# A table of 4722 queue edits laid over a planned two-layer attention and mixer kernel

## The chip, the core and the metric

The kernel runs on one core of a Trainium2 chip. The metric is the device time of one execution in microseconds. Inputs are given, outputs are one bf16 array of 2048 x 448.

## The reference

Sequence 2048, width 448, 16 heads of 28. Two blocks A and B, each applied twice with the same weights:

```python
def A(x):                                   # attention
    q, k, v = split(x @ wqkv)               # 16 heads of 28
    p = softmax(q @ k.T * 28 ** -0.5)
    return (p @ v) @ wo
def B(x):                                   # token mixer and MLP
    h = gelu(layernorm(x) @ w1)
    hs = shift_tokens_by_quarter(h) @ w2    # quarters moved by -1, +1, -2, +2 tokens
    x1 = x + hs
    return x1 + gelu(layernorm(x1) @ w3) @ w4      # 448 -> 1792 -> 448
x = x + A(layernorm(x)); x = x + B(layernorm(x))   # and both once more
```

## The kernel before, in words

Nothing in this kernel stands in a fixed program order. Some sixty small generators (`t_load`, `t_kv`, `t_scores`, `t_exp`, `t_pv`, `t_norm`, `t_outproj`, `t_mixA`, `t_mixB`, `t_w4` and so on) each yield operations with an engine, a planned duration, and the tiles that they read and write. `Sched.run` plays these against planned durations on the host while the kernel is built, and always records next the operation that it would start first; that record is a `Plan`. The order of a queue on the chip is the order in which its operations were recorded. `Plan.add` derives what each operation depends on, `Plan.finalize` turns that into semaphore waits, and `Plan.emit` writes the five queues (`pe`, `act`, `dve`, `pool`, `sp`). The plan has 11344 operations: 8083 on PE, 893 on ACT, 1552 on DVE, 454 on POOL and 362 on SP, which issues the DMAs.

The steps that matter here:

- **Scores** (`score_ops`, L1423). Queries are taken in chunks of 512 or 256 columns, keys in tiles of 128, heads in four groups of four. One score matmul multiplies a 28-wide (padded to 32) slice of keys with the queries; head j of a group lies in partitions 32j to 32j+31, so the matmul uses 32 rows of the array and all 128 columns, at `tile_position=(32 * j, 0)`. PSUM has eight banks. Score blocks go to banks 0, 1 and 2 for one unit and 3 and 4 for the next, in turn.
- **Exponentials** (`t_exp`, L1661). ACT takes a unit's three banks (1536 columns) or two banks (1024 columns) in one instruction and writes the tile `PT`. The scores of a unit wait until the unit before the last has been read out of its banks. Some blocks are sent to DVE instead, which makes the exponential in five steps (L1505, L1532, L1534, L1536, L1539; 97 blocks).
- **P times V** (`t_pv`, L819 through the helper `mm`). One matmul per key tile and head: 128 rows, and 32 columns of the array, its result in partitions 32j to 32j+31 of bank 5. The loop that records them has the head innermost:

```python
for kb in batch:
    for i, kt in enumerate(kbs[kb]):
        for j in range(4):
            yield op("pe", ..., mm(ps[32 * j:32 * j + 32, 5, 0:NW], vaug[...], buf[...], ...,
                                   tile_position=(0, 32 * j)), ...)
```

- **All other products** (L828 through the helper `mm4`): projections of q, k and v, the output projection, w1 to w4. Each operation emits four matmuls, one for each group of 32 columns.
- **Filler** (`keep_pe_busy`, L2151): 1006 operations of four matmuls on `ident`, put into PE's queue where the planner saw PE idle for long.
- On ACT besides the exponentials: the table changes and gelu of the MLP (L2105), tanh for the mixer's gelu (L1925), scale factors (L1368). On DVE: evacuation of PSUM, normalization, the update of the queries between key segments (L1445). On POOL: squares and normalization factors. On SP: weights, the round trips of the unnormalized output (`uscr`, `ub`), the broadcast of the reciprocal sums (`rscr`, `fb`), DMA transposes (L1038) and the output rows (L2140, two buffers `obf`).

Near the end, after the last exponential, there remain the last chunk's output projection and MLP: w3 and w4 products of 14 tiles, gelu on ACT and the output rows.

Of the kernel before, what the change touches and what calls it, by code (L numbers as in the profile page):

```python
# [13 lines left out]
U16 = mybir.dt.uint16  # L14

ENGS = ("pe", "act", "dve", "pool", "sp")


class _Op:
    __slots__ = ("eng", "fn", "deps", "sig", "cnt", "waits", "dma", "ekey", "vc", "sem", "t_end", "pos", "plan")  # L20

    def __init__(self, eng, fn, dma):
        self.eng = eng
        self.fn = fn
        self.deps = {}
        self.sig = False
        self.cnt = 0
        self.waits = ()
        self.dma = dma
        self.ekey = ("dma", id(self)) if dma else eng  # L30
        self.vc = None
        self.sem = None
        self.t_end = 0.0
        self.pos = 0


def _split(acc):
    if isinstance(acc, tuple) and len(acc) == 2 and isinstance(acc[0], tuple):
        return acc
    return acc, None  # L40


class Plan:
    def __init__(self):
        self.ops = {e: [] for e in ENGS}
        self.all = []
        self.track = {}
        self.listen = {}
        self.dirty = set()

    def deps(self, eng, reads, writes, extra=(), dma=False):
        out = {}

        def dep(d):
            if d is None:
                return
            if eng == "pe" and d.eng == "pe" and not d.dma and not dma:
                return
            cur = out.get(d.ekey)
            if cur is None or d.pos > cur.pos:  # L60
                out[d.ekey] = d

        for d in extra:
            dep(d)
        track = self.track
        for is_write, accs in ((False, reads), (True, writes)):
            for acc in accs:
                if len(acc) == 2 and type(acc[0]) is tuple:
                    key, part = acc
                else:  # L70
                    key, part = acc, None
                st = track.get(key)
                if st is None:
                    continue
                wl, rl = st
                psum = key[0] == "ps"
                for (o2, p2) in wl:
                    if part is None or p2 is None or part == p2 or (psum and (o2.eng != eng or o2.dma or dma)):
                        dep(o2)
                if is_write or psum:  # L80
                    for (o2, p2) in rl:
                        if (is_write and (part is None or p2 is None or part == p2)) or (psum and (o2.eng != eng or o2.dma or dma)):
                            dep(o2)
        return out

    def add(self, eng, fn, reads=(), writes=(), deps=(), dma=False, t_end=0.0):
        op = _Op(eng, fn, dma)
        op.pos = len(self.all)
        op.t_end = t_end
        op.deps = self.deps(eng, reads, writes, deps, dma)  # L90
        for is_write, accs in ((False, reads), (True, writes)):
            for acc in accs:
                key, part = _split(acc)
                st = self.track.get(key)
                ls = self.listen.get(key)
                if ls:
                    self.dirty |= ls
                if st is None:
                    st = self.track[key] = ([], [])
                wl, rl = st  # L100
                if is_write:
                    if part is None:
                        del wl[:]
                        del rl[:]
                    else:
                        wl[:] = [(o2, p2) for (o2, p2) in wl if p2 != part]
                        rl[:] = [(o2, p2) for (o2, p2) in rl if p2 != part]
                    wl.append((op, part))
                else:
                    rl[:] = [(o2, p2) for (o2, p2) in rl if not (o2.ekey == op.ekey and p2 == part)]  # L110
                    rl.append((op, part))
        self.ops[eng].append(op)
        self.all.append(op)
        return op

    def finalize(self, nc, stack):
# [3 lines left out]
        sems = {}  # L120
        for e in ENGS:
            sems[e] = stack.enter_context(nc.semaphore("sem_" + e))
            c = 0
            for op in self.ops[e]:
                if not op.dma and op.sig:
                    c += 1
                    op.cnt = c
                    op.sem = sems[e]
        known = {e: {} for e in ENGS}
        pool = []  # L130
# [54 lines left out]
class Sched:  # L185
# [12 lines left out]
    def __init__(self, P):  # L198
        self.P = P
        self.cur = {e: 0.0 for e in ENGS}  # L200
        self.runq = []
# [391 lines left out]
def build_kernel(nc, A_x, A_wqkv, A_wo, B_x, B_w1, B_w2, B_w3, B_w4, out, n_layers=2):  # L593
# [13 lines left out]
    NKV = 23  # L607
# [68 lines left out]
    P = Plan()  # L676
    SC = Sched(P)
    st = contextlib.ExitStack()
    with st:
        def sb(name, shape, dt):  # L680
            return st.enter_context(nc.sbuf_tensor(name, shape, dt))

        ps = st.enter_context(nc.psum_tensor("ps", [128, 8, 512], FP32))
        x_res = sb("x_res", [128, XR, D], FP32)
        obf = sb("obf", [128, 2, D], BF16)
        ones_bf = sb("ones_bf", [128, 128], BF16)
# [37 lines left out]
        vaug = sb("vaug", [128, NKV, 512], BF16)  # L724
# [58 lines left out]
        def op(eng, dur, fn, reads=(), writes=(), **kw):  # L783
            if eng == "pool" or (eng == "dve" and kw.pop("two", False)):
                kw["port"] = True
            if eng == "dve" and dur > 0.3:
                dur += 0.008
            return (eng, dur, fn, list(reads), list(writes), kw)
# [93 lines left out]
        def t_setup():  # L882
            yield op("dve", 0.1, lambda e: e.memset(ones_f[:, :], 1.0), writes=[("ones_f",)])
            yield op("dve", 0.15, lambda e: e.memset(ones_bf[:, :], 1.0), writes=[("ones_bf",)])
            yield ("spawn", t_setup_pool(), 0)
            yield ("spawn", t_setup_act(), 0)
            yield ("spawn", t_setup_ind(), 0)
            yield op("dve", 0.06, lambda e: e.memset(halfs[:, :], 0.5), writes=[("halfs",)])
            yield op("dve", 0.06, lambda e: e.memset(neghalf[:, :], -0.5), writes=[("neghalf",)])
            yield op("dve", 0.2, lambda e: e.memset(xn[:, :, D:512], 0.0), writes=[(("xn", i), "pad") for i in range(NXN)])  # L890
            yield ("sig", ("setup",))
            for (wp, nm) in ((wk_pad, "wk_pad"), (wq_pad, "wq_pad")):
                yield op("dve", 0.2, lambda e, wp=wp: e.memset(wp[:, :, :].rearrange("p c (h r) -> p c h r", r=32)[:, :, :, 28:32], 0.0), writes=[((nm,), "p")])
                yield op("dve", 0.27, lambda e, wp=wp: e.memset(wp[64:128, 3, :], 0.0), writes=[((nm,), "p")])
                yield ("spawn", t_pack(0 if nm == "wq_pad" else 1), 0)
            yield ("spawn", t_setup_late(), 2)
            yield ("spawn", t_setup2(), 4)
            yield ("spawn", t_ratio(), -1)
# [39 lines left out]
        def t_setup_act():  # L938
            pads = vaug[:, :, :].rearrange("p t (h r) -> p (t h) r", r=32)
            yield op("act", 1.4, lambda e: e.activation(out=pads[:, :, 28:32], in_=ones_bf[:, 0:4].unsqueeze(1).to_broadcast([128, 16 * NKV, 4]), func=ACT.Copy, scale=0.0),  # L940
                     reads=[("ones_bf",)], writes=[("vaug_all",)])
            yield op("act", 0.45, lambda e: e.activation(out=pads[:, :, 28:29], in_=ones_bf[:, 0:1].unsqueeze(1).to_broadcast([128, 16 * NKV, 1]), func=ACT.Copy),
                     reads=[("ones_bf",)], writes=[("vaug_all",)])
            yield ("sig", ("vinit",))

        wsts = [PT[:, 0:4, 0:D], PT[:, 4:8, 0:D]]
# [1248 lines left out]
        SC.spawn(t_final(), 9)  # L2195
        est = SC.run()

        P.finalize(nc, st)
        with nc.Block() as block:
            @block.sync  # L2200
# [23 lines left out]
def bass_interleave_layers__mha_block__mixer_s_mlp__prompt_kernel(nc, A_x, A_wqkv, A_wo, B_x, B_w1, B_w2, B_w3, B_w4, out):  # L2224
    build_kernel(nc, A_x, A_wqkv, A_wo, B_x, B_w1, B_w2, B_w3, B_w4, out)
# [28 lines left out]
```

## Time and profile before

| what | value |
|---|---|
| median of 3 runs | 1028.84 us (1028.56 to 1029.57) |
| profiled execution, its own time | 1027.68 us |
| span of that execution | 1026.0 us |
| granted TensorE clock | 1.000 throughout |
| first score matmul, last score matmul | 15.1 us, 973.45 us after the start |
| ACT, idle time in the windows from 25 to 950 us | 2.4 us |
| DMA | 62.64 MB, 61 GB/s mean |

The span is from the first to the last instruction of the profiled execution; its own time is taken by the device around that. Line numbers in the profile are those of the kernel before; in the changed kernel the same statements stand 678 lines lower (L819 is L1497, L828 is L1506, L1423 is L2101, L1661 is L2339; the filler's L2151 is L2829). PE is the matmuls, PEld the weight loads that go with them; both are issued from one queue. "x790" is a count of instructions, and a group's busy time counts overlapping instructions once.

### The profile page before, as it was taken

To read this page: it belongs to the slowest core of one execution; us is meant where nothing else is said; L and a number is where in the kernel's file an instruction comes from. 1 tells how busy PE (TensorE), PEld (TensorE's weight loads), DVE (VectorE), ACT (ScalarE), POOL (GpSimd) and SP (SyncE) were. 2 spreads that over 40 slices of the span, in tenths; PEclk is the share of its full clock that TensorE was granted. 3 is DMA by queue.
4 is the path that set the end of the run, shared out by engine and by line. 5 is a ranking of instruction groups with operands and counts; after the bars stand their busy time and mean duration, and the time that the engine had idled before them with its cause. 6 is when DMAs were issued, how large, how long until landed. Compare 5 with 4: busy or idle time off the path is not lost.

```text
span 1026.0 us, 37152 instructions
## 1 busy us (share of the span) xinstructions
PE 989.0 (96%) x16783; PEld 428.8 (42%) x16785; DVE 804.5 (78%) x1552; ACT 988.5 (96%) x907; POOL 289.6 (28%) x458
## 2 busy tenths in 40 slices
PE   8999999999999999999999999999999999999998
PEld 4332444444333244444433343433434443444465
DVE  8868899988888776876777687987897887786551
ACT  8999999999999999999999999999999999999952
POOL 3313011531433205242335122112534140522130
PEclk9999999999999999999999999999999999999999
DMA  4633242310221003121222024433302120121000
GB/s 126 150 108 112 73 107 71 63 39 24 55 66 44 12 23 99 29 59 28 49 88 60 12 81 127 136 85 94 71 24 38 44 43 13 34 69 31 13 16 29
DMA packets 99398, 62.64 MB, mean 61 GB/s; under 512 B 68712, under 2 KB 88552, under 8 KB 99240
## 3 DMA queue, kind: packets, MB, share of 16 engines
q1 hardware_dynamic: 99240, 60.27, 22.9%
q8 instruction: 131, 2.15, 0.9%
q14 instruction: 27, 0.22, 0.1%
HBM read 28.16 MB, written 16.76 MB: 44 GB/s over the span
## 4 chain that ended last, share of the span: by engine, by line
ACT 63%; PE 32%; DVE 3%; DMA 1%; issue 1%; POOL 0%; SPq 0%; DVEq 0%; ACTq 0%
ACT PT L1661 57%; PE ps L828 16%; PE ps L1423 8%; PE ps L819 5%; PE ps L2151 2%; ACT h2T L2105 2%; ACT fb L1925 1%; DMA fb<-rscr 1%; DVE fb L1532 1%; ACT L2105 1%; ACT L1661 1%; ACT kT L2105 0%; DMA PT<-in_A_wqkv_dram 0%; DVE fb L1534 0%; ACT vaug L2105 0%
## 5 line engine op out<-in xcount | busy, mean ns | idle before, releaser
L1661 ACT ACTIVATE PT<-ps 128x1024 bf16<-128x1024 f32 (+1 forms) x790 | 894.0, 1311 | 2.9 <-PE ps L1423 1.3
L1423 PE MATMUL ps<-qT,kT 32*128 32x512 bf16 (+1 forms) x2304 | 272.9, 335 | 17.4 <-ACT PT L1661 12.2
L819 PE MATMUL ps<-PT,vaug 128*32 128x512 bf16 (+1 forms) x2445 | 246.7, 341 | 0.0
L828 PE MATMUL ps<-xT,w 128*32 128x512 bf16 (+4 forms) x2816 | 187.7, 340 | 2.1 <-DVE h2T L2084 0.7
L2151 PE MATMUL ps<-ident 128*32 128x256 bf16 x4024 | 179.2, 277 | 1.7 <-POOL ident L913 1.5
L1423 PEld LDWEIGHTS ps<-qT,kT 32*128 32x128 bf16 x2304 | 70.8, 91 | 246.2 <-ACT PT L1661 219.7
L2151 PEld LDWEIGHTS ps<-ident 128*32 128x32 bf16 x4024 | 116.3, 97 | 34.0 <-issue 13.7
L819 PEld LDWEIGHTS ps<-PT,vaug 128*32 128x32 bf16 x2445 | 73.1, 95 | 90.2 <-issue 76.9
L828 PEld LDWEIGHTS ps<-xT,w 128*32 128x32 bf16 (+1 forms) x2816 | 77.1, 95 | 54.8 <-issue 24.6
L1505 DVE TENSOR_SCALAR yd<-ps 128x512 int32<-128x512 f32 x93 | 63.9, 687 | 23.3 <-PE ps L1423 22.6
L1768 POOL TENSOR_TENSOR otn<-ub,fb 128x512 bf16<-128x512 f32 (+1 forms) x28 | 33.2, 1187 | 157.8 <-DMA fb<-rscr 150.0
L828 PE MATMUL ps<-w,h2T 128*32 128x448 bf16 x1120 | 75.7, 354 | 0.9 <-ACT h2T L2105 0.4
L1532 DVE SCALAR_TENSOR_TENSOR fb<-yd 128x512 f32<-128x512 uint16 x93 | 70.9, 768 | 0.7
L1534 DVE SCALAR_TENSOR_TENSOR fb<-fb,yd 128x512 f32<-128x512 f32 x93 | 68.1, 735 | 0.5
L2084 DVE CAST h2T<-ps 128x512 bf16<-128x512 f32 (+1 forms) x71 | 45.1, 635 | 27.7 <-PE ps L828 26.6
L1539 DVE SCALAR_TENSOR_TENSOR PD<-yd,PD 128x512 int16<-128x512 int16 x93 | 64.4, 694 | 1.4
L1161 POOL TENSOR_TENSOR sq<-kT 128x512 bf16<-128x512 bf16 (+2 forms) x32 | 32.4, 1018 | 93.9 <-DVE kT L1175 82.3
L1161 POOL TENSOR_TENSOR sq<-qT 128x512 bf16<-128x512 bf16 x24 | 27.6, 1154 | 105.1 <-DVE qT L1220 99.9
L828 PE MATMUL ps<-xT,wq_pad 128*32 128x512 bf16 x512 | 44.9, 382 | 0.6 <-issue 0.5
L1536 DVE TENSOR_SCALAR PD<-fb 128x512 bf16<-128x512 f32 x94 | 41.6, 444 | 0.8
L828 PE MATMUL ps<-wo_pad,otn 128*32 128x448 bf16 x512 | 37.5, 355 | 4.1 <-DVE vaug L2077 1.6
L1423 PE MATMUL ps<-wk_pad,kT 32*128 32x512 bf16 x256 | 39.2, 385 | 1.8 <-ACT PT L1661 1.4
(196 smaller groups left out, 1227.0 us busy)
## 6 DMA issues: line engine op xcount, KB each, us to landing
uscr<-ub SPq DMA_DIRECT2D x28, 256.0 KB
ub<-uscr SPq DMA_DIRECT2D x28, 256.0 KB
fb<-rscr SPq DMA_DIRECT2D x24, 256.0 KB
xnd<-xn SPq DMA_DIRECT2D x28, 128.0 KB, 2.5
xd<-x_res SPq DMA_DIRECT2D x16, 224.0 KB, 3.9
x_res<-xd SPq DMA_DIRECT2D x16, 224.0 KB
w<-in_B_w_dram SPq DMA_DIRECT2D x5, 448.0 KB, 8.2
obf<-in_A_x_dram SPq DMA_DIRECT2D x16, 112.0 KB
```

The lines of the kernel that those rows point to most:

```text
L819: return lambda e: e.matmul(out=out, lhsT=lhsT, rhs=rhs, start=start, stop=stop, **kw)
L828: r.append(e.matmul(out=out[c:c + w, :], lhsT=lhsT[:, c:c + w], rhs=rhs, start=start, stop=stop, tile_position=(0, c)))
L1161: return both("sq", 0.15 + NW * 0.0018, 0.07 + NW * 0.00104, lambda e: e.tensor_tensor(out=sq[:, si, 0:NW], in0=src, in1=src, op=ALU.mult) ...
L1423: yield op("pe", (0.005 + NW * 0.00042) / nc_, lambda e, i=i, kc=kc, j=j, g=g, qt=qt, a=a, NW=NW, bank=bank: e.matmul(out=ps[:, bank, i * ...
L1505: yield op("dve", c_ps(512), lambda e: e.tensor_scalar(out=y, in0=ps[:, bi(bank), :], scalar1=SCALE * L2E * FS, scalar2=-126.0 * FS, op0=A ...
L1532: yield op(D_[0][0], D_[0][1], lambda e: e.scalar_tensor_tensor(out=q, in0=lo, scalar=E2 / E3 * FS, in1=lo, op0=ALU.add, op1=ALU.mult), re ...
L1534: yield op(D_[1][0], D_[1][1], lambda e: e.scalar_tensor_tensor(out=q, in0=q, scalar=E1 / E3 * FS * FS, in1=lo, op0=ALU.add, op1=ALU.mult) ...
L1536: yield op(D_[2][0], D_[2][1], lambda e: e.tensor_scalar(out=pdt, in0=q, scalar1=E3 / FS ** 3, scalar2=E0, op0=ALU.mult, op1=ALU.add), rea ...
L1539: yield op(D_[3][0], D_[3][1], lambda e: e.scalar_tensor_tensor(out=pdt.bitcast(I16), in0=hi, scalar=128.0, in1=pdt.bitcast(I16), op0=ALU. ...
L1661: yield op("act", 0.069 + n * w * 0.000833, lambda e, bk=bk, s0=s0, n=n, w=w: e.activation(out=PT[:, s0:s0 + n, 0:w], in_=ps[:, bk[0]:bk[0 ...
L2084: ev = op("dve", c_ps(m * NW), lambda e, hr=hr, pv=pv: e.tensor_copy(out=hr, in_=pv), reads=[("ps", bi(b))], writes=hk, touch=[b])
L2151: return [e.matmul(out=ps[32 * c:32 * c + 32, bi(b), 0:256].rearrange("p (a n) -> p a n", n=128), lhsT=ident[:, 32 * c:32 * c + 32], rhs=i ...
```

## The change

After the planner has run, its five queues are taken apart and put together again by a table. An entry (a, b) names two operations by the place in which the planner recorded them: all the a are taken out of their queues, and then, entry by entry, a is put right behind b on the same engine. 3953 entries are for PE, 478 for DVE, 129 for POOL, 126 for SP and 36 for ACT. `rearranged` then records all operations anew, in an order that every queue and every earlier dependency allows, so that `finalize` derives waits and semaphores for the new order. To know which operations must stay ahead of which, `add` keeps all readers and writers of a tile (`hist`, `need`). One set of declared writes grows (the padding of V).

```diff
+MOVES = (
+    (113, 89), (114, 90), (78, 114), (76, 78), (82, 76), (77, 82), (75, 77), (80, 75), (81, 80), (102, 81), (99, 102),
...
+)
 class Plan:
...
+    def rearranged(self, moves):
+        n = len(self.all)
+        nxt, prv = {}, {}
...
+        for (a, b) in moves:
+            p, q = prv[a], nxt[a]
+            nxt[p] = q
+            if q is not None:
+                prv[q] = p
+        for (a, b) in moves:
+            q = nxt[b]
+            nxt[b], prv[a], nxt[a] = a, b, q
+            if q is not None:
+                prv[q] = a
+        heads = [nxt[-1 - k] for k in range(len(ENGS))]
+        new = Plan()
+        made = [None] * n
+        for _ in range(n):
+            best = None
+            for k, h in enumerate(heads):
+                if h is not None and (best is None or h < heads[best]) and all(made[d] is not None for d in self.need[h]):
+                    best = k
...
+            h = heads[best]
+            eng, fn, reads, writes, deps, dma, t_end = self.args[h]
+            made[h] = new.add(eng, fn, reads, writes, [made[d.pos] for d in deps if d is not None], dma, t_end)
+            heads[best] = nxt[h]
+        return new
...
             yield op("act", 0.45, lambda e: e.activation(out=pads[:, :, 28:29], ...),
-                     reads=[("ones_bf",)], writes=[("vaug_all",)])
+                     reads=[("ones_bf",)], writes=[("vaug_all",)] + [("vaug", s) for s in range(NKV)])
...
         est = SC.run()
+        P = P.rearranged(MOVES)
         P.finalize(nc, st)
```

As an example, this is one stretch of PE's queue before and after, near the end; a number is the column group j of a P times V matmul, M a product of four matmuls:

```
before  M M M M 0 1 2 3 0 1 2 3 0 1 M M M 2 3 0 1 2
after   M M M M M M M M M M 1 3 0 3 3 0 3 2 2 1 1 2
```

## The prediction

> **What bounds the kernel now.** I read the page first (busy shares, the chain that ended last, the costliest groups), then the waits, a stretch of the chain, and single rows of the timeline. From the page:
>
> ```profile
> span 1026.0 us, 37152 instructions
> PE 989.0 (96%) x16783; PEld 428.8 (42%) x16785; DVE 804.5 (78%) x1552; ACT 988.5 (96%) x907; POOL 289.6 (28%) x458
> ...
> ACT 63%; PE 32%; DVE 3%; DMA 1%; issue 1%; POOL 0%; SPq 0%; DVEq 0%; ACTq 0%
> ...
> L1661 ACT ACTIVATE PT<-ps 128x1024 bf16<-128x1024 f32 (+1 forms) x790 | 894.0, 1311 | 2.9 <-PE ps L1423 1.3
> L1423 PE MATMUL ps<-qT,kT 32*128 32x512 bf16 (+1 forms) x2304 | 272.9, 335 | 17.4 <-ACT PT L1661 12.2
> L819 PE MATMUL ps<-PT,vaug 128*32 128x512 bf16 (+1 forms) x2445 | 246.7, 341 | 0.0
> ...
> L2151 PE MATMUL ps<-ident 128*32 128x256 bf16 x4024 | 179.2, 277 | 1.7 <-POOL ident L913 1.5
> ```
>
> PE and ACT both look full, but a matmul's 0.34 us overlaps its neighbours. Who waits for whom tells them apart (us in total, times, longest):
>
> ```profile
> PEld ps L1423 <- ACT PT L1661: 248.9, 687, 1.2
> ```
>
> PE's queue stands before the next score matmuls until an exponential has emptied their banks, 687 times. So ACT sets the pace and PE has room. Its pace is in the chain (start, length):
>
> ```profile
> 817.96 69.25 ACT PT L1661 x62
> ```
>
> That is 1.117 us each: exponentials start 1.330 us apart behind a 1536-wide one and 0.904 behind a 1024-wide one. Of all 790, 84 start later than that, by 13.1 us together. So a perfect order has 13.1 us to win here, and little at the ends.
>
> **What PE's matmuls cost each other.** Each uses a quarter of the array: the score matmuls (L1423) one group of 32 rows, the P·V matmuls (L819) one group of 32 columns; a projection (L828) or filler (L2151) is four matmuls, one to each column group. Rows of the timeline (start, length, matmuls):
>
> ```profile
> 302.65 0.39 PE L819 MATMUL ps<-PT,vaug 128*32 128x512 bf16 x3
> ...
> 206.07 0.59 PE L819 MATMUL ps<-PT,vaug 128*32 128x512 bf16 x5
> ...
> 963.38 0.39 PE L1423 MATMUL ps<-qT,kT 32*128 32x256 bf16 x6
> ...
> 390.88 0.60 PE L1423 MATMUL ps<-qT,kT 32*128 32x256 bf16 x6
> ```
>
> Three P·V matmuls on three groups take as long as one, 0.39; five take 0.21 more, since the fifth goes to the group of the first. Six scores on three row groups take 0.39, two rounds; the six at 390.88 fall four on one group and two on another and take 0.60. Their starts there are 390.885, .888, 391.004, .008, .113 and .222: the fifth is for a group free since 390.995 and still waits behind the fourth. So three rules, from this trace: matmuls start in queue order; one waits until the last on its group is through (0.213 us for 512 columns, 0.107 for 256); and between scores and the rest everything drains and 0.105 us passes (scores at 302.97, next matmul at 303.286).
>
> **The change, part by part.** No operation is added or taken away. The built order after holds the same matmuls, the same 790 exponentials in the same sequence and the same 14 table loads. So ACT's work is unchanged; what moves is who stands ahead of whom.
>
> PE, the dear part. The planner sends P·V matmuls to column groups 0,1,2,3 in turn: before, no two neighbours in the queue share a group. After, 617 neighbouring pairs do (300 of 512 columns, 317 of 256), and a further 241 meet their group again at distance two or three. In turn, four of them share 0.213 us; behind one of its own group, each takes 0.213 alone. The pairs cost up to 300 x 0.160 + 317 x 0.080 = 73 us, the 241 about 16 more, and neighbours on other groups give some back. Score pairs on one row group go from 9 to 211: 18 of 512 and 193 of 256 columns, 24.5 us, against 1.2 before. P·V runs are cut from 537 into 742 pieces; mode changes go from 1585 to 1596, 1.2 us.
>
> Summing PE's queue from its first to last matmul by the three rules, with no waits for other engines, gives 964 us before and 1082 after: +118, of which 76 from P·V groups, 24 from score groups, 18 from the cut runs. From the first score to the last it is 904 before (the trace: 15.1 to 973.45, 958; the other 54 are waits) and 1022 after. The table compares PE's sum in that stretch with ACT's own pace, over 39 blocks of 20 exponentials:
>
> | | PE | ACT | blocks where PE is longer |
> |---|---|---|---|
> | before | 894 | 925 | 9 |
> | after | 1011 | 925 | 39 |
>
> The 54 us of waiting hid PE's work before; 118 more is over twice that. So the bound changes sides: ACT waits for scores, everywhere.
>
> What waiting stays inside PE's 1022? Between nothing (always late) and 54 (as before). Taking in blocks of four exponentials the longer of PE and ACT gives 20 us over PE's own sum; the same reckoning for before gives 959 where the trace has 952, a little high. I take 18. The ends stay: 15.1 until the first score; 52.55 from the last score to the span's end, where the queue sum is 49.6 in both orders. Span: 15.1 + 1022 + 18 + 52.55 = 1108. The profiled execution took 1027.68, 1.7 above its span; the median of the runs, 1028.84, is 1.2 above that. So 1111.
>
> The other engines I cost at nothing. DVE (1063 of 1552 places changed) is busy 78%; its largest move, the query update L1445 by up to 50 places (26 us at 804.5/1552 each), had 43 us until its first reader, and the two that had only 1.4 and 1.6 us move by two places at most. SP's 274 moved DMAs and POOL's 301 (28% busy) move by three places on average; past the first 7 us no wait row names either as ACT's releaser. ACT changes 112 places, mostly small L1925 and L1368 operations past an exponential. Semaphore waits stay alike (PE 1559 before, 1546 after), so no engine queues behind new ones. If that cover failed, it would add to 1111; what PE's lateness frees speaks against it. Start and end: between -3 us (transposes no longer behind the column sums at 8.57) and +3 (output tiles finishing in a bunch, two output buffers); I take 0.
>
> **A rule that makes it dearer.** In the rows, projections follow each other on the same groups every 0.18 to 0.21 us though their weight loads (PEld, 95 ns) come between: the loads hide. The Trainium skill ("TensorE: Matmul & The Clock Gate", Part 3, The mechanism) says that a weight load overlaps matmuls in flight only when the row group differs, which would bare a load in each same-group pair; this trace disagrees for column groups.
>
> **The rivals.**
> - *Bare weight loads.* Each of the 828 pairs also pays a load of 0.095: +79, 1190 us. For: only 9 such pairs of scores are in the trace before, and none of P·V. Against: the pair at 390.885 costs 0.119, not 0.107 + 0.095.
> - *Half hidden.* Neighbours on free groups, or weights loaded early, halve the 118: PE's sum is 1023, its stretch 963, with 54 of waits partly kept; about 1060. Against: the fifth score at 391.113 waited.
> - *The array goes around a busy group* (the other side). If a matmul on a free group passes a blocked one, order within a run is free, PE's sum stays near 965, under ACT's pace, and what is left of the change is timelier scores: at best the 13.1 us of late exponentials go, 1016. It decides once PE's sum stays under about 1000. For: four starts 3 ns apart look independent. Against: the same score at 391.113.
> - *Gaps.* The stretches of other work between scores that are over 1 us grow from 55 to 122, the longest in mid-kernel from 2.3 to 4.6; with two banks' worth of scores in hand, each may stop ACT though the sum fits. If a third of a microsecond of each of the 67 more is bare, that alone is +20, 1050; it lies inside the forecast's waiting.
> - *The change isn't what it says.* The built order shows the moves; no chance.
>
> **How the numbers follow.** PE in order 0.78, at 1111; half hidden 0.10; bare loads 0.05; going around 0.07, of which 0.02 ends level. Gaps alone have no chance of their own. The forecast's own range is 1092 (no waiting) to 1147 (54). Stretched down a good half of the way to the half-hidden case, it is 1080 to 1150; that leaves out bare loads, going around and part of the half. A measurement of this kernel tells about 0.2% (2 us; the runs lie within 1.0) from no change: faster 0.05, same 0.02, slower 0.93.
>
> **What would show it.** Right: PE's share of the chain rises past ACT's; the wait of L1423 for ACT falls well under 249 us and ACT's idle before L1661 grows from 2.9; 62 exponentials take about 75 us where they took 69; timeline rows of four P·V matmuls last over 0.5 us; MATMUL counts stay. Wrong: ACT still starts every 1.117 us (going around), or same-group pairs are 0.2 us apart at 256 columns (bare loads), or DVE or DMA ends ACT's waits.

## The result and the profile after

| | median | runs | profiled execution | span | first to last score |
|---|---|---|---|---|---|
| before | 1029.29 us | 5, 1028.56 to 1029.57 | 1027.68 | 1026.0 | 15.12 to 973.45 |
| after | 1081.34 us | 5, 1079.43 to 1081.89 | 1079.43 | 1077.7 | 15.34 to 1025.56 |

The ratio is 1.0503, 95% interval 1.0488 to 1.0519: 52 us slower. The forecast was 82 slower, with a range that holds 1081 near its low end. The ends are as they were (15.3 us ahead of the first score, 52.1 after the last); the 52 us lie between. The page of the kernel after, the lines that answer to those shown of before (a group's line: busy us, mean ns of one, idle time before and what ended it):

```profile
span 1077.7 us, 37143 instructions
PE 1050.3 (97%) x16785; PEld 474.3 (44%) x16785; DVE 808.6 (75%) x1552; ACT 1011.7 (94%) x907; POOL 282.4 (26%) x458
...
PE 76%; ACT 16%; DVE 7%; issue 1%; DMA 0%; SPq 0%; POOL 0%; DVEq 0%; ACTq 0%
...
L2339 ACT ACTIVATE PT<-ps 128x1024 bf16<-128x1024 f32 (+1 forms) x790 | 914.5, 1228 | 30.8 <-PE ps L2101 22.9
L1497 PE MATMUL ps<-PT,vaug 128*32 128x512 bf16 (+1 forms) x2445 | 337.6, 339 | 1.6 <-DVE ub L2422 1.0
```

The chain that ended last has changed hands: ACT 63% and PE 32% before, PE 76% and ACT 16% now. The exponentials' idle time grew from 2.9 to 30.8 us. Their busy time grew from 894.0 to 914.5, because an exponential that starts late no longer overlaps the one before it: 27.9 and 20.5 make 48 of the 52 us. By single rows, 288 exponentials start later than ACT's pace allows, by 60.8 us together (before: some 85, by 13.1); the 62 in one piece of the chain of before, which took 69 us, take 74.2. The P·V matmuls have the same mean length, 339 ns, but lie beside each other less: their busy time as a group rose from 246.7 to 337.6. From the waits ("issue" is time in which the queue waited for nothing that the profile shows):

```profile
PEld ps L2101 <- issue: 168.0, 532, 0.4
...
PEld ps L2101 <- ACT PT L2339: 94.9, 259, 1.2
```

PE stood 248.9 us before scores for an exponential to empty their banks, 687 times; now 94.9, 259 times. Of the timeline's rows of four P·V matmuls, 25 of 52 last over 0.5 us, where 7 of 45 did. All this is what the prediction named as its signs, and less of it than forecast. One stretch shows why (timeline, start, length, matmuls):

```profile
130.67 0.39 PE L2101 MATMUL ps<-qT,kT 32*128 32x512 bf16 x2 [0.19 <-ACT PT L2339]
130.98 0.39 PE L1497 MATMUL ps<-PT,vaug 128*32 128x512 bf16 x1
130.99 0.29 PE L2829 MATMUL ps<-ident 128*32 128x256 bf16 x3
131.11 0.48 PE L1497 MATMUL ps<-PT,vaug 128*32 128x512 bf16 x4
...
132.07 0.39 PE L2101 MATMUL ps<-qT,kT 32*128 32x512 bf16 x3
```

In the queue, this stretch has P·V matmuls on column groups 1, 1, 1, then a filler (one matmul on each group), 2, 3, 3, 0, and two fillers. The three on group 1 stand first; yet right after the first P·V matmul start three of the filler's, which are behind the other two in the queue: those on the free groups. From the first matmul at 130.98 to the next score at 132.07 is 1.082 us by the single records. Queue order would give 1.493. The load of group 1 alone, three times 0.213 and three times 0.107, plus 0.105, gives 1.066.

So the first rule of the prediction looked wrong, and one of its rivals right. **The theory after the result:** matmuls go around a busy group, and a stretch between two drains (changes between row and column groups) costs its most loaded group plus 0.105 us, in whatever order it is queued. **The rival:** they start in queue order, as predicted, and the rest was hidden by PE's room.

The two can be laid over the whole trace after. In 189 of its stretches on column groups the two rules differ by over 0.08 us. Together these took 219 us; the most loaded group gives 212, queue order 262; 183 of them were shorter than queue order allows by over 0.03 us. Summed from first to last score:

| kernel | PE's sum, most loaded group | first to last score | the rest: waits |
|---|---|---|---|
| before | 904 | 958 | 54 |
| after | 963 | 1010 | 47 |

### The profile page after: what moved, and what is told of

Its sections match the earlier page's. It is cut to its first block, busy times and chain, and to the rows that moved or that the text cites. A ratio compares the mean times of both kernels' runs of the same rounds, so it can differ in the third digit from the quotient of the medians.

```text
span 1077.7 us, 37143 instructions
## 1 busy us (share of the span) xinstructions
PE 1050.3 (97%) x16785; PEld 474.3 (44%) x16785; DVE 808.6 (75%) x1552; ACT 1011.7 (94%) x907; POOL 282.4 (26%) x458
## 4 chain that ended last, share of the span: by engine, by line
PE 76%; ACT 16%; DVE 7%; issue 1%; DMA 0%; SPq 0%; POOL 0%; DVEq 0%; ACTq 0%
PE ps L1506 31%; PE ps L2101 20%; PE ps L1497 17%; ACT PT L2339 13%; PE ps L2829 8%; ACT h2T L2783 1%; DVE fb L2210 1%; DVE PD L2217 1%; DVE ub L2422 1%; DVE PD L2214 1%; DVE fb L2212 0%; DVE kT L1853 0%; DVE yd L2183 0%; DMA PT<-in_A_wqkv_dram 0%; DVE x_res L2503 0%
## 5 line engine op out<-in xcount | busy, mean ns | idle before, releaser
L2339 ACT ACTIVATE PT<-ps 128x1024 bf16<-128x1024 f32 (+1 forms) x790 | 914.5, 1228 | 30.8 <-PE ps L2101 22.9
L1497 PE MATMUL ps<-PT,vaug 128*32 128x512 bf16 (+1 forms) x2445 | 337.6, 339 | 1.6 <-DVE ub L2422 1.0
L2101 PE MATMUL ps<-qT,kT 32*128 32x512 bf16 (+1 forms) x2304 | 288.3, 335 | 8.3 <-ACT PT L2339 6.9
L1506 PE MATMUL ps<-xT,w 128*32 128x512 bf16 (+3 forms) x2816 | 187.6, 340 | 2.5 <-DVE hT L2575 1.4
L2829 PE MATMUL ps<-ident 128*32 128x256 bf16 x4024 | 183.6, 278 | 2.2 <-POOL ident L1591 1.5
L2101 PEld LDWEIGHTS ps<-qT,kT 32*128 32x128 bf16 x2304 | 76.0, 91 | 236.9 <-issue 144.4
L1497 PEld LDWEIGHTS ps<-PT,vaug 128*32 128x32 bf16 x2445 | 118.2, 95 | 98.9 <-issue 58.9
L2829 PEld LDWEIGHTS ps<-ident 128*32 128x32 bf16 x4024 | 113.6, 97 | 44.1 <-issue 25.0
L1506 PE MATMUL ps<-xT,wq_pad 128*32 128x512 bf16 x512 | 42.6, 382 | 0.4 <-DVE qT L1927 0.2
L1506 PEld LDWEIGHTS ps<-w,h2T 128*32 128x32 bf16 x1120 | 30.7, 96 | 24.4 <-issue 8.3
```

Of the source, the lines that this page charges most:

```text
L1497: return lambda e: e.matmul(out=out, lhsT=lhsT, rhs=rhs, start=start, stop=stop, **kw)
L1506: r.append(e.matmul(out=out[c:c + w, :], lhsT=lhsT[:, c:c + w], rhs=rhs, start=start, stop=stop, tile_position=(0, c)))
L2101: yield op("pe", (0.005 + NW * 0.00042) / nc_, lambda e, i=i, kc=kc, j=j, g=g, qt=qt, a=a, NW=NW, bank=bank: e.matmul(out=ps[:, bank, i * ...
L2339: yield op("act", 0.069 + n * w * 0.000833, lambda e, bk=bk, s0=s0, n=n, w=w: e.activation(out=PT[:, s0:s0 + n, 0:w], in_=ps[:, bk[0]:bk[0 ...
L2829: return [e.matmul(out=ps[32 * c:32 * c + 32, bi(b), 0:256].rearrange("p (a n) -> p a n", n=128), lhsT=ident[:, 32 * c:32 * c + 32], rhs=i ...
```

## The experiments

**The rule by itself.** A small kernel issues patterns to single groups (c0 is a matmul on column group 0, and so on), with a matmul of the other kind between them:

```diff
+COLS = ("0123", "00123", "000123", "0000123", "00000123", "0000000123", "00112233", "000111222333", ...)
+for p in COLS:
+    for _ in range(3):
+        row_mark(e, ps, w, x)
+        for c in p:
+            col[int(c)](e, ps, w, x, 512)
```

> A small kernel by itself (it computes nothing of the reference): after 320 matmuls to warm up, patterns of matmuls on column groups 0 to 3 (512 columns, 0.213 us each on its group) and on row groups (256 columns, 0.107 us), three times each, with one matmul of the other kind between them, so that everything drains. Queue order, as the prediction read it: in 0 0 0 1 2 3 the first matmul on group 1 starts 0.426 us after the first of all; 00112233 lasts 1.065 us, 000111222333 1.917, and eight on 0 followed by eight on 1 3.195. Going around a busy group: group 1 starts within 0.02 us of the first in 000123 and 0000123 alike; 00112233 lasts 0.426, 000111222333 0.639, eight and eight 1.704. In between, if only one matmul may wait for each group: group 1 starts at 0.213 us in 000123 and at 0.426 in 0000123; if two may wait, at 0 and 0.213; and so on, which tells how far it looks. Row groups the same at half the times.

Its timeline, for 000123 and for 0000000123 (L44 is the mark; L12, L16, L20 and L24 are groups 0, 1, 2 and 3):

```profile
24.67 0.23 PE L44 MATMUL ps<-x,w 32*128 32x128 bf16 x1
24.83 0.39 PE L12 MATMUL ps<-x,w 128*32 128x512 bf16 x1
24.84 0.39 PE L16 MATMUL ps<-x,w 128*32 128x512 bf16 x1
...
25.05 0.59 PE L12 MATMUL ps<-x,w 128*32 128x512 bf16 x2
...
33.88 0.22 PE L44 MATMUL ps<-x,w 32*128 32x128 bf16 x1
34.03 1.04 PE L12 MATMUL ps<-x,w 128*32 128x512 bf16 x4
34.70 0.39 PE L16 MATMUL ps<-x,w 128*32 128x512 bf16 x1
...
34.91 0.81 PE L12 MATMUL ps<-x,w 128*32 128x512 bf16 x3
```

In 000123, group 1 starts 0.010 us after the first of all and 0.22 ahead of the second on group 0, which is ahead of it in the queue. In 0000123 it is 0.013. With five on group 0 ahead, group 1 starts just after the second of them (0.23), and with seven just after the fourth (0.664, the last row but one). So three may wait on a group behind the one at work; the next for the same group holds up all that follow. 000111222333 is through after three rounds (its last starts at 0.471), where queue order needs nine. Eight and eight is limited by that depth: group 1 starts at 0.88, as soon as the fifth on group 0 does. On row groups, 0000123 has its second group start at 0.013 as well. The Trainium skill ("TensorE: Matmul & The Clock Gate", Part 3, The mechanism) says that matmuls start and end strictly in queue order; these rows disagree for starts, and the measurement decides. The ends are modelled in the profile, so nothing is shown of them.

**The rule in the kernel.** Before's queues, with the P·V matmuls of each unbroken run sorted by column group:

```diff
+        queues = dict(planned)
+        queues['pe'] = self.runs(queues['pe'], self.is_pv, self.by_group)
```

> All queues as before, but in each unbroken run of P times V matmuls on PE those of one column group follow each other (0 0 1 1 2 2 3 3 where it was 0 1 2 3 0 1 2 3). Nothing crosses another operation. Queue order: PE's sum from the first score to the last rises from 904 to 975 us; taking the longer of PE and ACT in blocks of four exponentials, 44 us more, so 1073 (at least 1055). Going around a busy group: the most loaded group of each stretch is the same, 904, so 1029 within 3; with only one matmul waiting for each group 912, so 1029 to 1037.

1030.22 us, ratio 1.0011 (1.0002 to 1.0020). Page and waits of this kernel (its statements lie 755 lines lower than in before):

```profile
L2416 ACT ACTIVATE PT<-ps 128x1024 bf16<-128x1024 f32 (+1 forms) x790 | 894.6, 1303 | 4.1 <-PE ps L2178 1.7
```

```profile
PEld ps L2178 <- ACT PT L2416: 243.2, 672, 1.2
```

The exponentials wait 4.1 us where they waited 2.9, and PE still stands 243 us for them. Neighbours on one group cost 1 us, not 44. So the order inside a run is not what costs; what is left is which groups the run holds, and that is tried next.

**How much the loads cost.** After's queues, with each P·V matmul sent to the least loaded group of its stretch; and the converse, before's queues with most of group 3's sent to group 0:

```diff
+            if self.is_pv(p):
+                g = min(range(4), key=lambda k: (round(load[k], 3), k))
+                self.relabel(p, g)
```
```diff
+            if self.is_pv(p):
+                self.relabel(p, 0 if self.group(p) == 3 and not first else self.group(p))
```

> All queues as after the change, but every P times V matmul is sent to the column group that has least to do in its stretch between two drains, whichever head it belongs to, and starts its own sum (so the output isn't the attention's; places, sizes and waits stay). With a matmul that goes around a busy group, a stretch costs its most loaded group plus 0.105 us; by that PE's sum from first to last score is 904 before, 963 after, 916 here. If the sum is all that counts, it gives back 47 of the 52 us: 1035. If the places of the scores among the other work (long stretches without scores) carry the loss: 1081. Playing the five queues with the durations of the trace of before and that rule gives spans of 1033 for before (1026 measured), 1089 for after (1078) and 1056 here: 32 us less than after, so 1049; that would mean some 30 from groups and some 20 from places.

> All queues as before, but P times V matmuls of column group 3 (but the first of each unit's sum) go to group 0 instead, each starting its own sum (so the output isn't the attention's). Places stay as before; PE's sum rises from 904 to 957, about as far as the change raised it. If the groups' loads alone carry the loss: 1029 + 52 = 1081, like after. Playing the queues as for the kernel above: 35 more than before, 1064. If PE's room of 54 us hides the rise: 1029 to 1035.

Balanced: 1047.75 us, ratio 1.0170 (1.0153 to 1.0187). Skewed: 1065.06, ratio 1.0341 (1.0326 to 1.0357). The chain of the balanced kernel, then of the skewed one:

```profile
ACT 48%; PE 41%; DVE 7%; DMA 2%; issue 1%; SPq 0%; POOL 0%; DVEq 0%; ACTq 0%
```

```profile
PE 78%; ACT 13%; DVE 6%; DMA 1%; POOL 1%; issue 1%; SPq 0%; DVEq 0%; ACTq 0%
```

Skewing alone, with every operation in its old place, turns before's chain into that of after. Balancing alone gives ACT half of it back. In both, some two thirds of the change in PE's sum reach the time: 53 us of sum cost 36, 47 less give 34. The remaining third is taken from PE's waits (54 to 40 in the skewed kernel, 47 to 62 in the balanced one).

So 34 of the 52 us are P·V's group loads, and 18 remain. After balancing, PE's sum is still 12 above before's, 10.5 of it in score matmuls that share a row group; at two thirds that is 8. Some 10 us are then left for the places of the scores among the other work. The other way round gives 12: after is 16 us dearer than the skewed kernel with a sum only 6 higher. That last part was only estimated so, not tried by itself.

**Which queues.** PE's edits alone, and the other four queues' edits alone:

```diff
+        queues = dict(planned, pe=edited['pe'])
```
```diff
+        queues = dict(edited, pe=planned['pe'])
```

> PE's queue as after the change, the other four as before it (9 of 8083 operations on PE jump ahead, so that the queues can run). If PE's queue alone carries the loss, as the prediction says: 1081 within 5. If the moves on DVE, SP, POOL and ACT carry the part that a recount of PE leaves over (PE's sum with free order inside a stretch rises by 59 us, and by 31 where ACT's pace is taken into account in blocks of four, against 52 measured): about 1060.

> PE's queue as before, the other four as after. By the prediction (the other engines cost nothing): 1029 within 3. If they carry what the recount of PE leaves over: about 1050.

PE alone: 1107.6 us, ratio 1.0741 (1.0703 to 1.0778). The others alone: 1062.9, ratio 1.0324 (1.0304 to 1.0343). Both expectations missed, on the dear side: 78 and 34 us, against 52 for the two together. PE's sums are 963 and 904, as they should be; it is the waits that grew, to 69 and 88 us. The exponentials of the kernel with PE's edits alone, then of the one with the others' alone:

```profile
L2415 ACT ACTIVATE PT<-ps 128x1024 bf16<-128x1024 f32 (+1 forms) x790 | 916.7, 1228 | 50.6 <-PE ps L2177 41.7
```

```profile
L2415 ACT ACTIVATE PT<-ps 128x1024 bf16<-128x1024 f32 (+1 forms) x790 | 898.0, 1272 | 27.5 <-PE ps L2177 25.2
```

A small part is the clock. With PE's edits alone, the three runs at a granted clock of 0.992 to 0.995 took 1107.2 to 1109.1 us, and the one at 1.000 took 1101.8. With the others' alone, all four runs are at 0.990 to 0.995; a straight line through them gives 1058 at full clock, an estimate. So some 73 and 29 us are left of the 78 and 34. One of the waits, from the timeline of the kernel with the others' edits alone (its statements lie 754 lines lower than in before):

```profile
660.35 0.39 PE L1573 MATMUL ps<-PT,vaug 128*32 128x512 bf16 x1
660.49 0.69 DVE L2259 TENSOR_SCALAR yd<-ps 128x512 int32<-128x512 f32 x1 [2.28 <-PE ps L2177]
...
661.10 0.68 DVE L2288 SCALAR_TENSOR_TENSOR fb<-fb,vaug 128x512 f32<-128x512 f32 x1
661.81 0.43 DVE L2290 TENSOR_SCALAR PD<-fb 128x512 bf16<-128x512 f32 x1
662.27 0.69 DVE L2293 SCALAR_TENSOR_TENSOR PD<-vaug,PD 128x512 int16<-128x512 int16 x1
...
663.02 0.39 PE L1573 MATMUL ps<-PD,vaug 128*32 128x512 bf16 x1 [2.29 <-DVE PD L2293]
```

DVE's edited queue stands 2.28 us at the first step of a block whose scores PE issues in its unedited place. Then come the block's other steps. PE's queue already stands at the P·V matmul that reads the result, 2.29 us, and the next scores are behind that. Right behind this wait the granted clock is at half from 663.8 to 670.6 us, so the clock's part may itself come of such waits. This is one wait of many; how many of the others are of its kind was not counted. The two sets of edits follow each other: given PE's, the others save 26 us (20 against the run at full clock).

**Without the fillers.** All 1006 fillers left out, of after and of before, and then only 626 of after:

```diff
+        gone = set(p for p in edited['pe'] if self.is_filler(p))
+        queues['pe'] = [p for p in queues['pe'] if p not in gone]
```
```diff
+        gone = set(self.long_gaps(edited['pe'], 1.0))
```

> As after the change without the 1006 fillers of four matmuls (they compute nothing). PE's sum falls by 119 us to 844, under ACT's pace of 925. If PE's sum as a whole sets the time, as the prediction had it: ACT's pace, so 1029 to 1040. If single stretches set it, with the rest of the queue having room: 1066 (playing the queues gives 15 us less than after). If the granted clock falls without them, PE slower by that share: above 1081.

> As before the change without the 1006 fillers. PE's sum falls from 904 to 785. With the clock granted in full all the time: 1027 (ACT sets the time). If the clock falls without them: slower, by the share of it that PE's stretches show.

> As after the change, but without those 626 fillers that stand in a stretch of PE's queue, between one score and the next, of more than 1.0 us by the loads of its groups. PE's sum falls from 963 to 898. If PE's sum sets the time at the rate that the balanced and the skewed kernel showed (about 0.7 us of time for each us of sum): 46 less than after, 1035. If the other work in those stretches (P times V and projections) is what makes scores late, and fillers only lie where there is room: playing the five queues gives 11 less, 1070. If the clock falls with fewer fillers, as without any: above 1081.

After: 1100.6 us, ratio 1.0684 (1.0645 to 1.0723), granted clock 0.938 in the profiled execution. Before: 1067.2, ratio 1.0359 (1.0334 to 1.0384), clock 0.910. The row of the granted clock in 40 slices, of before without fillers:

```profile
PEclk9999777788979898999899999889678999899999
```

With them the row is 9 throughout. Taking 119 us of work off PE made both kernels slower, by 19 and 38 us: the fillers hold the clock. The traces agree with the Trainium skill ("TensorE: Matmul & The Clock Gate", Part 1, What's actually happening), which says that the clock is granted by how busy PE has been recently. As a test of PE's sum the two say nothing.

With 626 left out: 1076.9 (1073.9 to 1085.9), ratio 1.0475 (1.0435 to 1.0514). The clock was 0.975 in the profiled execution, the slowest of the four, and 0.986 to 0.992 in the others. That excludes the 1035 of a time set by PE's sum as a whole: even all of it at 0.975 would be 1062. It doesn't settle whether there is a gain, since the clock fell too; a straight line through the four times and clocks gives 1069 at full clock, an estimate near the expected 1070.

**A queue made by the new rule.**

```diff
+        queues['pe'] = [planned['pe'][i] for a, b in SLICES for i in range(a, b)]
```

> All operations as before and the other four queues as before; PE's queue is a permutation of before's, found by trying small moves (up to ten operations past a group of scores, or one to four operations by up to twelve places) and keeping those that shorten the play of the five queues with the durations of the trace of before and the rule that a matmul goes around a busy group. By that rule PE's sum is 905 (904 before) and fewer exponentials start late; the play gives 10 us less than before, so 1019 to 1027. If matmuls started in queue order, PE's sum would rise by 25 to 930 and the time to about 1040. If the play is no better than its own error of 1%: anything between 1020 and 1040.

1030.08 us, ratio 1.0008 (0.9999 to 1.0017): no gain. The 10 us that the play of the queues promised lie within its own error, and no version here beats the kernel before. But this queue has 25 us more than before's when counted in queue order (1 more by loads), and that costs nothing either. Its P·V matmuls are busy as a group for 284.5 us, where before's are for 246.7: such a rise is no price by itself.

## Why the prediction was right about the sign and wrong about the size

- **The step that failed: "matmuls start in queue order; one waits until the last on its group is through".** The second half holds: the patterns show 0.215 us between matmuls of 512 columns on one group. The first half came from a misread row. At 390.885 the queue holds scores on row groups 3, 2, 3, 3, 2, 3. The prediction took the starts to be in that order, so that the start at 391.113 was the fifth score's, kept waiting on a free group. A row of the timeline doesn't tell the group. With group 2's second score going around, it is the start at 391.008, and every one of the six starts when its own group is free.
- **PE's term, +118, is +59** (964 to 1023 over the whole queue; 904 to 963 between the scores). By loads, column-group stretches give 47, scores 10.5 and mode changes 1.2, where the prediction had 76 for P·V pairs, 24 for scores and 18 for cut runs. A pair of neighbours is no cost. A run cut so that it holds two of one group and none of another is.
- **The waiting, 18, is 47.** The longer of PE and ACT in blocks of four, done again with the right rule, gives 995 where the trace has 1010; no run shows why it falls short. The two errors, 59 too much and 29 too little, leave the 30 us between 1111 and 1081. The forecast's own range began at 1092 and misses; the stated one held because its low end was stretched towards a case that assumed half the cost. For the size, that was luck.
- **"The bound changes sides: ACT waits for scores, everywhere".** The side is right, "everywhere" isn't: by loads PE is longer in 28 of the 39 blocks of 20, and 288 of the 790 exponentials start late.
- **The ends and the time beside the span** held: 15.34 and 52.1 us, and 1.7.
- **"The other engines cost nothing"** was argued from the margins of single moves. Held against PE's old queue the same moves cost 34 us, an estimated 29 at full clock. It holds only in the sense that they go with PE's. (The largest move on DVE is of 83 places, not 50: a copy at L1953, for which nothing waits in either trace.)
- **The rivals.** Going around had the right mechanism and the wrong price. It took order to be all that had changed and kept PE's sum near 965, while the make-up of the runs had changed with it and the sum went to 1023. Half hidden named 1023 and 963, the right sums, but by halving the cost; the runs show no half-hidden pairs, only order that is free and loads that are not. Bare weight loads are excluded: same-group matmuls follow each other at 0.215 us, with loads of about 0.098 between them. The gaps were given 20 us, and 10 to 12 are what the other terms leave.

## What to carry to other kernels

Where matmuls use quarters of the array, count for each stretch between two drains the work of every group, and price the stretch by the most loaded one: order inside it is nearly free here as long as no more than four in a row share a group, an uneven share is not. To read an order rule off a trace, issue a pattern whose groups can be told apart by line, since a row of the timeline doesn't name the group. And price edits of several queues together: half of them alone can cost more than all.

## What the runs showed of the hardware that was not expected

- Matmuls on a free group start ahead of earlier ones in the queue that wait for a busy group: 0.010 us after the first of all in 000123. Three can wait behind the one at work on a group; a fifth in a row on one group stops the queue until the second has started (0.23 us).
- Without fillers, PE is still busy 89% of the span in before, and the granted clock falls to 0.910 on average.
- In the small kernel the clock went to half at 62.3 us, while the profile shows no gap on PE, among patterns in which mostly one group of 32 rows was at work. Patterns with one group of 32 columns at work just before had kept it at full. The cause was not tried.
